# A planner learns what tile shapes cost: charges on TensorE, a 1e-9 moved to ScalarE, a new order

## The chip, the cores and the metric

The kernel runs on one core of one Trainium2 chip. The metric is the device time of one execution in microseconds. Five engines work side by side, each through its own queue in order: TensorE (PE; PEld is its weight load), VectorE (DVE), ScalarE (ACT), GpSimd (POOL) and SyncE (SP, which issues most DMAs). They wait for one another through semaphores only.

## The reference, cut to what matters

```python
# 1. attention: 4 batches, 8 heads, 576 rows, head size 64, rotary embedding on q and k
scores = scale * np.matmul(q_rot, k_rot.transpose(0, 1, 3, 2))
attn = np.exp(scores - np.max(scores, axis=-1, keepdims=True))
attn = attn / (np.sum(attn, axis=-1, keepdims=True) + 1e-09)
x = (attn @ v)                              # laid out as 2304 tokens x 512
# 2. a layer with SoLU and layer norm, 512 -> 1024 -> 512
h = x @ w_in
e = np.exp(h - h_max)
solu = h * (e / (np.sum(e, axis=-1, keepdims=True) + 1e-09))
x = ((solu - mu) / np.sqrt(var + 1e-06) * g_ln) @ w_out
# 3. experts: tokens with x @ w_skip > 0 go to the expert of their largest logit
out = x + gate * (np.maximum(x @ w1[e], 0.0) @ w2[e])
```

## The kernel before, in words

Every float32 product is made from two halves: a rounded high part and the rest, so one product is three matmuls (high x high, high x low, low x high). ScalarE makes the high part, VectorE the low one.

Attention goes over 16 pairs of heads (4 batches x 4). A pair loads q, k and v, applies the rotary embedding on GpSimd or VectorE (L475 to L487), transposes the result on TensorE (L503, L506), splits it (L532, L535) and has a DMA swap the halves of q (L560). Then it goes through 5 chunks of query rows (`chunk`). Chunks 0 to 3 hold 128 rows of both heads, chunk 4 the last 64 rows of each. For each head of a chunk: the scores (`score`, L595, 64-row tiles of TensorE, into one of two PSUM buffers S), their negated maximum (L598, VectorE), the exp with its sum (L601, ScalarE). Then, once for the chunk, VectorE adds 1e-9 to the sums (L610) and takes the reciprocal (L611), and each head's row block is scaled by it on ScalarE (L619), VectorE (L621) or GpSimd (L623). TensorE transposes the blocks (L661; for chunk 4 in 64-row tiles, L638), ScalarE or VectorE evict them (L668, L670), and TensorE multiplies by v (L700, 128 x 64 tiles, "pv").

The second layer goes over 18 tiles of 128 tokens (`solu`): w_in matmuls (L748), maximum, exp, product, statistics, a power on GpSimd (L777), the layer norm's scaling (L782, then L788 on ScalarE or L790 on VectorE or GpSimd), transposes (L802) and splits, w_out matmuls (L823), the output rows, and the routing of the tile's tokens, which ends in a scatter of rows by GpSimd (L899). The weights are turned into high and low parts on the way. When the last tile is routed, tables are made and a loop over expert tiles follows (L1053 to L1080), whose code is written by hand, outside the plan; two expert tiles of the fullest early expert are planned as filler for the end.

What sets the order: every step up to there is registered by `op(engine, kind, function, reads, writes, priority)` with a class `Plan`. `Plan.run` plays the steps on five engines: a step's duration comes from `COST`, the delay between engines from `LAT`, the buffers from `CAPS`; an engine that is free takes the ready step of lowest priority number whose buffers are free. The order in which it takes them is the program: `emit` writes it out, engine by engine. `TUNE` holds the priorities' offsets (`lead`, `sb`, `so`, `lt` and others) and lists that choose an engine for a step: `rp` (rotary embedding), `nr` (scaling: 0 GpSimd, 1 ScalarE, 2 VectorE), `ev` (eviction: 0 VectorE, 1 ScalarE), `ln` (layer norm: 0 GpSimd, 1 ScalarE, 2 VectorE), `xg`, `xs`, `le`, `wh`, `wl` (smaller copies). `BETWEEN` names the VectorE kinds that the plan lets start only when GpSimd isn't holding the data port they share, and `HOLDS` the GpSimd kinds that hold it. On the chip nothing of the plan is left but the order in each queue.

Of the kernel before, what the change touches and what calls it, by code (L numbers as in the profile page):

```python
# [9 lines left out]
F32 = mybir.dt.float32  # L10
# [4 lines left out]
AF = mybir.ActivationFunctionType  # L15
ALU = mybir.AluOpType
# [5 lines left out]
    "w_ld": (450, 1456), "c_ld": (2250, 1200), "w_1": 335, "w_2": 602, "w_r": 520, "w_add": 1250, "w_log": 663, "rope3": 1560, "ropev3": 790, "w_hi": 613, "w_lo": 663, "w_loP": 1225, "w_hiv": 400,  # L22
    "qk_ld": (450, 819), "v_ld": (2400, 910), "ropev": 680, "rope": 1393, "prep4": 430, "prep1": 107,
    "st_hi": 605, "st_lo": 700, "st_hi1": 160, "st_lo1": 230, "st_hi2": 278, "st_lo2": 447, "q2_ld": (1250, 1638),
    "score": 480, "score2": 960, "max": 665, "exp": 717, "rec": 278, "norm": 724, "normA": 667, "normv": 429, "h_lnA": 1130, "h_lnv": 723,
    "T10": 650, "DVE_ev5": 480, "ACT_ev5": 430, "T4": 436, "T1": 107, "ACT_ev4": 478, "DVE_ev4": 602, "DVE_ev1": 198, "ACT_ev1": 160, "pv": 2320, "x_hi2": 265, "x_lo2": 335, "pvs": 870,
    "DVE_ev1": 198, "x_hi": 160, "x_lo": 202, "mm3": 696, "mm1": 235, "h_max": 1140, "h_exp": 1120, "h_u": 1140, "h_bn": 600,
    "h_st": 805, "h_pow": 700, "h_mu": 70, "h_ln": 1190, "c_hi": 478, "c_lo": 602, "xs_ev": 478, "x_st": (1250, 730),
    "lg": 356, "g_sum": 120, "g_max": 80, "g_exp": 250, "g_hot": 927, "g_gate": 340, "rank": 140, "g_acc": 70, "g_ix": 477,
# [9 lines left out]
    'ld': 106.36,  # L39
    'ldv': 102.14,  # L40
    'rope': -9.86,
    'qk': 1.92,
    'sl': 0.88,
    'pvl': 6.39,
    'sper': 11.03,
    'hq': 31.3,
    'lt': -81.75,
    'rt': 5.62,
    'ew': 191.41,
    'olag': 1,  # L50
    'direct': 1,
    'c': -67.39,
    'lead': [136.53, 2.97, 6.06, 5, 9.68, -2.38, 8.75, 5.34, -1.45, -2.08, 8.42, 4.99, 0.81, 14.63, 7.23,
# [32 lines left out]
BETWEEN = {"w_1", "w_2", "w_hiv", "w_log", "normv", "h_lnv", "h_st", "h_mu", "g_hot", "g_ix"}  # L86
HOLDS = {"rope", "rope3", "norm", "w_add", "w_loP", "h_ln", "r_xP", "xf_loP"}
# [14 lines left out]
class Plan:  # L102
# [38 lines left out]

    def run(self):
        ops, lat = self.ops, self.lat
# [6 lines left out]
        room = {t: [(0, x) for x in range(n)] for t, n in self.caps.items()}  # L150
# [4 lines left out]
        rt = [0] * len(ops)  # L155
        ev = [(0, o.i) for o in ops if not o.nd]
        ev += [(t, -1) for t in busy.values()]
        heapq.heapify(ev)
        now, hw, dm = 0, 0, self.start.get("DMA", 0)
        held = free = 0  # L160
        seq = []
        while len(seq) < len(ops):
# [5 lines left out]
            for e, h in ready.items():  # L168
# [3 lines left out]
                while h:  # L172
                    x = heapq.heappop(h)
                    need = {}
                    for f in ops[x[1]].alloc:
                        need[f.tag] = need.get(f.tag, 0) + 1
                    if all(sum(y[0] <= now for y in room[t]) >= n for t, n in need.items()):
                        got = ops[x[1]]
                        break
                    skip.append(x)  # L180
# [12 lines left out]
                if not isinstance(c, tuple):  # L193
                    s0 = now
                    if o.kind in BETWEEN:
                        s0 = max(now, held)
                    elif o.kind in HOLDS:
                        s0 = max(now, free)
                    o.t1 = busy[e] = s0 + c * (2 if e == "PE" and now < self.warm else 1)
                    if o.kind in BETWEEN:  # L200
                        free = o.t1
                    elif o.kind in HOLDS:
                        held = o.t1
                elif e == "SP":
                    busy[e] = hw = max(hw, now) + c[0]
                    o.t1 = dm = max(dm, hw + 650) + c[1]
                    out = self.dma
                else:
                    busy[e] = now + c[0]
                    o.t1 = busy[e] + c[1]  # L210
# [31 lines left out]
def kern(ctx, tc, q, k, v, w_in, w_out, g_ln, w_skip, w_gate, w1, w2, cs, ids, out):  # L242
    nc = tc.nc
    P = 128
# [18 lines left out]
    eps = cst.tile([P, 4], F32, name="eps")  # L263
# [172 lines left out]
    def pair(n):  # L436
# [145 lines left out]
        def chunk(c):  # L582
# [26 lines left out]
            def rec(nx=nx):  # L609
                nc.vector.tensor_tensor(sr[:, 0:nx], sr[:, 0:nx], eps[:, 0:nx], op=ALU.add)  # L610
                nc.vector.reciprocal(sr[:, 0:nx], sr[:, 0:nx])  # L611

            op("DVE", "rec", rec, r=[(sr, x) for x in range(nx)], w=[(sr, "r")], pri=ps_)
# [705 lines left out]
```

## Time and profile before

| | us |
|---|---|
| three runs | 710.41, 710.58, 705.21 (median 710.41) |
| the profiled execution's own time | 709.91 |
| its span, first to last instruction | 708.0 |
| TensorE busy | 648.4 (92%) |
| VectorE busy | 512.4 (72%) |
| ScalarE busy | 369.9 (52%) |
| GpSimd busy | 251.6 (36%) |

The busy shares are means over stages that differ: attention alone at first, attention with the second layer in the middle, experts at the end. A matmul's end is modelled, so TensorE's pace is read from the starts of its instructions. The granted clock says how much of TensorE's full speed the chip allowed in a stretch; 0.5 is the lower level.

### The profile page before, as it was taken

The numbers are of one execution on the slowest core, as the hardware profiler recorded it, in microseconds if no ns is written. First come the engines' busy times: TensorE is split into PE (matmuls) and PEld (weight loads), VectorE is DVE, ScalarE is ACT, GpSimd is POOL, SyncE is SP. The second block draws the span as 40 slices with busy tenths as digits, with TensorE's granted clock in tenths as the row PEclk, the third lists the DMA queues.
The fourth block names the chain that finished last, engine by engine and source line by source line (L and its number), as shares of the span: only waits on it lengthen the run. The fifth ranks groups of instructions, "written<-read, shape, count | busy, mean of one in ns | idle before, by whom it ended". The sixth has DMA issues, their size and how long they took to land. (4 is left out here: it accounts for less than half of the span.)

```text
span 708.0 us, 12918 instructions
## 1 busy us (share of the span) xinstructions
PE 648.4 (92%) x4588; PEld 487.6 (69%) x4588; DVE 512.4 (72%) x1265; ACT 369.9 (52%) x845; POOL 251.6 (36%) x266
## 2 busy tenths in 40 slices
PE   2888978979999999999999999999999969898994
PEld 1655656757777777777776777777777757677773
DVE  5899889999888778888788779768677845224411
ACT  2777767678535556655475475855345421123311
POOL 5985735463214816205013403213112231421230
PEclk9998889999999999999999999999999989999998
DMA  4624334442212322111221201200136110440000
GB/s 136 171 79 140 87 96 117 124 112 80 62 33 54 88 50 62 36 49 37 53 73 31 67 1 45 64 19 1 23 74 175 45 45 16 160 178 31 18 32 11
DMA packets 42188, 49.10 MB, mean 69 GB/s; under 512 B 27508, under 2 KB 27636, under 8 KB 42112
## 3 DMA queue, kind: packets, MB, share of 16 engines
q1 hardware_dynamic: 39744, 44.43, 23.5%
q0 software_dynamic: 2368, 3.74, 1.7%
q8 instruction: 38, 0.62, 0.4%
q14 instruction: 38, 0.31, 0.2%
HBM read 38.50 MB, written 6.99 MB: 64 GB/s over the span
## 5 line engine op out<-in xcount | busy, mean ns | idle before, releaser
L601 ACT ACTIVATE P<-S,nm 128x576 f32<-128x576 f32 x144 | 106.5, 741 | 39.3 <-DVE nm L598 31.2
L598 DVE TENSOR_REDUCE nm<-S 128x1 f32<-128x576 f32 x144 | 106.4, 748 | 11.9 <-PE S L595 9.5
L823 PE MATMUL A<-woh,lh 128*128 128x512 f32 x288 | 110.6, 421 | 0.0
L595 PE MATMUL S<-k,qa 64*128 64x288 f32 x576 | 100.2, 324 | 4.0 <-ACT P L601 1.9
L661 PE MATMUL T<-ident,P 128*128 128x128 f32 x576 | 88.8, 287 | 11.3 <-ACT ptall L668 4.4
L700 PE MATMUL T<-ptall,vt 128*64 128x256 f32 (+2 forms) x960 | 95.5, 344 | 2.6 <-DVE qa L535 1.3
L661 PEld LDWEIGHTS T<-ident,P 128*128 128x128 f32 x576 | 67.1, 144 | 33.5 <-ACT ptall L668 7.2
L595 PE MATMUL S<-k,qb 64*128 64x288 f32 x384 | 83.5, 333 | 1.9 <-ACT P L601 1.7
L595 PEld LDWEIGHTS S<-k,qa 64*128 64x128 f32 x576 | 70.2, 191 | 18.6 <-issue 9.2
L700 PEld LDWEIGHTS T<-ptall,vt 128*64 128x64 f32 (+1 forms) x960 | 56.8, 140 | 33.5 <-issue 8.3
L668 ACT ACTIVATE ptall<-T 128x512 f32<-128x512 f32 (+1 forms) x117 | 57.2, 507 | 37.0 <-PE T L661 33.9
L623 POOL TENSOR_SCALAR P<-P,sr 128x576 f32<-128x576 f32 x43 | 36.3, 846 | 102.6 <-DVE sr L611 61.7
L595 PEld LDWEIGHTS S<-k,qb 64*128 64x128 f32 x384 | 57.0, 194 | 14.1 <-issue 5.9
L823 PEld LDWEIGHTS A<-woh,lh 128*128 128x128 f32 x288 | 54.7, 190 | 15.6 <-issue 4.6
L748 PE MATMUL S<-wih,xth 128*128 128x512 f32 x144 | 60.3, 419 | 0.0
L823 PE MATMUL A<-wol,lh 128*128 128x512 f32 x144 | 56.7, 394 | 0.0
L748 PE MATMUL S<-wih,xtl 128*128 128x512 f32 x144 | 56.4, 392 | 0.0
L748 PE MATMUL S<-wil,xth 128*128 128x512 f32 x144 | 56.3, 391 | 0.0
L475 POOL TENSOR_TENSOR rt<-raw,csq 128x576 f32<-128x576 f32 x23 | 33.6, 1462 | 62.0 <-PE T L506 40.2
L619 ACT ACTIVATE P<-P,sr 128x576 f32<-128x576 f32 x60 | 45.5, 775 | 14.3 <-DVE sr L611 12.1
L670 DVE COPY ptall<-T 128x512 f32<-128x512 f32 (+1 forms) x75 | 37.7, 518 | 10.2 <-PE T L661 8.8
L899 POOL DMA_INDIRECT srt<-gi,ix x18 | 19.6, 1091 | 70.7 <-DVE ix L896 38.5
(228 smaller groups left out, 1288.0 us busy)
## 6 DMA issues: line engine op xcount, KB each, us to landing
qb<-qa SPq DMA_DIRECT2D x30, 256.0 KB, 3.7
raw<-in_q SPq DMA_DIRECT2D x16, 288.0 KB, 2.9
raw<-in_k SPq DMA_DIRECT2D x16, 288.0 KB, 3.9
out<-xs SPq DMA_DIRECT2D x36, 128.0 KB, 2.4
s<-in_moe_w_in SPq DMA_DIRECT2D x8, 512.0 KB, 5.1
s<-in_moe_w_out SPq DMA_DIRECT2D x8, 512.0 KB, 3.7
st<-in_moe_w SPq DMA_DIRECT2D x8, 512.0 KB, 4.6
w1r<-in_moe_w SPq DMA_DIRECT2D x4, 1024.0 KB, 8.2
```

The lines of the kernel that those rows point to most:

```text
L475: e.tensor_tensor(t1[:, 0:NJ].rearrange("p j (e i) -> p j e i", e=2), raw.t.rearrange("p j (e i) -> p j e i", e=2), c, op=ALU.mult)
L595: nc.tensor.matmul(sp[:, bank, 0:288], lhsT=l, rhs=r_, start=first, stop=fin)
L598: nc.vector.tensor_reduce(nm[:, x:x + 1], sp.t[:, :, 0:288], AX.XY, ALU.max, negate=True)
L601: nc.scalar.activation(pt[:, x * S:(x + 1) * S].rearrange("p (a b) -> p a b", a=2), sp.t[:, :, 0:288], AF.Exp, bias=nm[:, x:x + 1], accum_ ...
L619: nc.scalar.activation(y, y, AF.Copy, scale=sr[:, x:x + 1])
L623: nc.gpsimd.tensor_scalar(y, y, sr[:, x:x + 1], 1.0, op0=ALU.mult, op1=ALU.mult)
L661: nc.tensor.transpose(tp.t[:w_, (y - g0) * P:(y - g0) * P + P], pt[:, y * P:y * P + w_], ident)
L668: nc.scalar.activation(ov, iv, AF.Copy)
L670: nc.vector.tensor_copy(ov, iv)
L700: nc.tensor.matmul(xp.t[64 * h:64 * h + 64, 0:M], lhsT=l, rhs=r_, start=(i == 0), stop=(i == 4))
L748: nc.tensor.matmul(hp[:, hf], lhsT=a, rhs=bb, start=(kc == 0 and y == 0), stop=(kc == KC - 1 and y == 2))
L823: nc.tensor.matmul(ob.t, lhsT=lh[:, a, kc], rhs=bb[:, kc], start=(kc == 0 and y == 0), stop=(kc == FC - 1 and y == 2))
```

## The change

Three things. The plan charges TensorE for a change of tile shape: `SHAPE` gives the kinds their shape (r: 64-row tiles, c: column tiles, m: full matmuls of the split weights, f: all others, the transposes), `CHANGE` the nanoseconds for going from one to the other, and where the tuned number `stick` is not 0, TensorE takes a ready step whose shape costs nothing ahead of the first ready one, if its priority number is at most `stick` higher. `BETWEEN` gains three kinds, `HOLDS` loses two that no step uses. The addition of 1e-9 to the softmax sums is an Identity activation with a bias operand on ScalarE. The costs and all of `TUNE` are drawn anew, and with them the order of the whole plan.

```diff
...
+    'stick': 0.5,
...
-    'ln': [1, 2, 0, 0, 2, 0, 0, 0, 2, 2, 2, 0, 0, 2, 1, 1, 1, 0],
+    'ln': [1, 0, 1, 2, 2, 1, 0, 2, 1, 2, 1, 1, 1, 1, 2, 1, 2, 1],
...
-BETWEEN = {"w_1", "w_2", "w_hiv", "w_log", "normv", "h_lnv", "h_st", "h_mu", "g_hot", "g_ix"}
-HOLDS = {"rope", "rope3", "norm", "w_add", "w_loP", "h_ln", "r_xP", "xf_loP"}
+BETWEEN = {"w_1", "w_2", "w_hiv", "w_lo", "w_log", "ropev", "ropev3", "normv", "h_lnv", "h_st", "h_mu", "g_hot", "g_ix"}
+HOLDS = {"rope", "rope3", "norm", "w_add", "w_loP", "h_ln"}
+
+SHAPE = {"score": "r", "score2": "r", "T10": "r", "pv": "c", "pvs": "c", "lg": "c", "mm3": "m", "mm1": "m", "rank": "m", "tab2": "m"}
+CHANGE = {"fm": -80, "fr": 94, "fc": 94, "mr": 178, "mc": 178, "rf": 92, "rm": 92, "rc": 92}
...
+                if e == "PE" and stick:
+
+                    rest = sorted(h)
+                    fit = [x for x in rest if self.fits(ops[x[1]], room, now)]
+                    same = [x for x in fit if CHANGE.get(last + SHAPE.get(ops[x[1]].kind, "f"), 0) <= 0]
+                    if fit:
+                        x = same[0] if same and same[0][0] <= fit[0][0] + stick else fit[0]
...
+                    if e == "PE":
+                        y = SHAPE.get(o.kind, "f")
+                        s0 += CHANGE.get(last + y, 0)
+                        last = y
...
             def rec(nx=nx):
-                nc.vector.tensor_tensor(sr[:, 0:nx], sr[:, 0:nx], eps[:, 0:nx], op=ALU.add)
                 nc.vector.reciprocal(sr[:, 0:nx], sr[:, 0:nx])
 
-            op("DVE", "rec", rec, r=[(sr, x) for x in range(nx)], w=[(sr, "r")], pri=ps_)
+            op("ACT", "s_eps", lambda nx=nx: nc.scalar.activation(sr[:, 0:nx], sr[:, 0:nx], AF.Identity, bias=eps[:, 0:1]),
+               r=[(sr, x) for x in range(nx)], w=[(sr, "e")], pri=ps_)
+            op("DVE", "rec", rec, r=[(sr, "e")], w=[(sr, "r")], pri=ps_)
```

Of the 144 entries of `nr` that are used, GpSimd has 43 before and 57 after, ScalarE 60 and 45, VectorE 41 and 42. Of the 128 evictions of four blocks ScalarE has 84 before and 73 after, VectorE 44 and 55. Of the 18 layer norms GpSimd has 8 before and 2 after, ScalarE 4 and 10, VectorE 6 and 6.

## Rows read from the trace of the kernel before

**Rows 1.** The page, part 1: busy us (share of the span) and instructions.
```profile
PE 648.4 (92%) x4588; PEld 487.6 (69%) x4588; DVE 512.4 (72%) x1265; ACT 369.9 (52%) x845; POOL 251.6 (36%) x266
```
**Rows 2.** Busy time by stretch: length, busy us by engine (instructions), granted clock, DMA share, GB/s.
```profile
40.00:80.00 40.00, 33.69 (x286) 23.41 (x284) 36.23 (x68) 29.49 (x72) 27.29 (x22) 0.87 0.36 110
80.00:120.00 40.00, 34.15 (x306) 23.52 (x306) 36.45 (x69) 30.66 (x78) 20.99 (x19) 0.91 0.40 104
280.00:360.00 80.00, 80.00 (x637) 59.91 (x636) 66.54 (x162) 44.20 (x107) 19.02 (x22) 1.00 0.21 52
560.00:580.00 20.00, 13.29 (x78) 10.15 (x77) 11.16 (x42) 6.25 (x13) 10.57 (x13) 0.92 0.16 40
```
**Rows 3.** TensorE's waits from 20 to 120 us: total us, times, longest.
```profile
PE T L661 <- ACT ptall L668: 3.7, 5, 1.1
```
**Rows 4.** TensorE's timeline: start us, us, what (first and last 64-row visit too).
```profile
14.57 0.60 PE L595 MATMUL S<-k,qa 64*128 64x288 f32 x1 [1.34 <-ACT k L532]
...
304.24 1.09 PE L661 MATMUL T<-ident,P 128*128 128x128 f32 x8
305.26 1.06 PE L595 MATMUL S<-k,qa 64*128 64x288 f32 x12
306.25 1.20 PE L661 MATMUL T<-ident,P 128*128 128x128 f32 x9
...
322.87 0.66 PE L661 MATMUL T<-ident,P 128*128 128x128 f32 x4
323.46 0.40 PE L595 MATMUL S<-k,qa 64*128 64x288 f32 x1
...
324.05 0.50 PE L823 MATMUL A<-woh,lh 128*128 128x512 f32 x1
...
508.77 0.52 PE L638 MATMUL T<-ident,P 64*128 64x64 f32 x10
```
**Rows 5.** Lines L610, L611: min/median/max ns; then L610's busy time by stretch.
```profile
L610 DVE TENSOR_TENSOR sr<-sr,eps x80: 139/154/1399, 20.0 to 496.7; 128x2 f32<-128x2 f32 x64, 128x1 f32<-128x1 f32 x16
...
L611 DVE RECIPROCAL sr<-sr x80: 163/166/167, 21.4 to 496.9; 128x2 f32<-128x2 f32 x64, 128x1 f32<-128x1 f32 x16
...
0.00:708.00 708.00, 28.20 (x80) 0.97 0.26 69
40.00:160.00 120.00, 11.86 (x24) 0.93 0.38 106
```
**Rows 6.** Timeline of all engines from 65.5 to 76 us.
```profile
67.30 1.31 DVE L610 TENSOR_TENSOR sr<-sr,eps 128x2 f32<-128x2 f32 x1
...
69.05 4.53 PE L700 MATMUL T<-ptall,vt 128*64 128x256 f32 x20 [1.27 <-DVE qa L535]
```
**Rows 7.** Groups of instructions by shape: busy us, mean ns | idle before.
```profile
L619 ACT ACTIVATE P<-P,sr 128x576 f32<-128x576 f32 x60 | 45.5, 775 | 14.3 <-DVE sr L611 12.1 <-DVE sr L610 2.0
L623 POOL TENSOR_SCALAR P<-P,sr 128x576 f32<-128x576 f32 x43 | 36.3, 846 | 102.6 <-DVE sr L611 61.7 <-ACT qa L532 7.9 <-DVE rt L866 7.1
L790 POOL TENSOR_SCALAR s<-s,st 128x1024 f32<-128x1024 f32 x8 | 9.6, 1203 | 2.2 <-DVE st L782 2.1
L871 ACT ACTIVATE rt<-rt,sc 128x8 f32<-128x8 f32 x18 | 5.3, 294 | 14.2 <-DVE sc L869 14.1
L788 ACT ACTIVATE s<-s,st 128x1024 f32<-128x1024 f32 x4 | 5.0, 1242 | 6.4 <-DVE st L782 6.4
L716 ACT ACTIVATE xth<-T 128x64 fp32r<-128x64 f32 x16 | 3.6, 223 | 1.8 <-PE T L700 1.6
```
**Rows 8.** Timeline from 569.5 to 583 us, TensorE and the others, at the plan's end.
```profile
569.59 0.16 DVE L782 SCALAR_TENSOR_TENSOR st<-st 128x1 f32<-128x1 f32 x1 [0.21 <-POOL st L778]
...
576.80 0.98 POOL L899 DMA_INDIRECT srt<-gi,ix  x1 [1.89 <-DMA srt<-gi,ix]
577.82 1.20 POOL L790 TENSOR_SCALAR s<-s,st 128x1024 f32<-128x1024 f32 x1
...
579.07 1.97 PE L802 MATMUL T<-ident,s 128*128 128x128 f32 x8 [4.35 <-POOL s L790]
```

More of the change, by code (lines that the diff above doesn't have):

```diff
@@ L21 @@
 COST = {
-    "w_ld": (450, 1456), "c_ld": (2250, 1200), "w_1": 335, "w_2": 602, "w_r": 520, "w_add": 1250, "w_log": 663, "rope3": 1560, "ropev3": 790, "w_hi": 613, "w_lo": 663, "w_loP": 1225, "w_hiv": 400,
+    "w_ld": (450, 1456), "c_ld": (2250, 1200), "w_1": 336, "w_2": 602, "w_r": 520, "w_add": 1240, "w_log": 663, "rope3": 1780, "ropev3": 860, "w_hi": 613, "w_lo": 590, "w_loP": 1225, "w_hiv": 400,
     "qk_ld": (450, 819), "v_ld": (2400, 910), "ropev": 680, "rope": 1393, "prep4": 430, "prep1": 107,
[L24 to L27, printed above, removed]
+    "st_hi": 494, "st_lo": 600, "st_hi1": 160, "st_lo1": 198, "st_hi2": 278, "st_lo2": 447, "q2_ld": (1250, 1638),
+    "score": 502, "score2": 900, "max": 665, "exp": 717, "rec": 166, "norm": 724, "normA": 667, "normv": 429, "h_lnA": 1130, "h_lnv": 723,
+    "s_eps": 170, "T10": 327, "DVE_ev5": 465, "ACT_ev5": 385, "T4": 436, "T1": 107, "ACT_ev4": 478, "DVE_ev4": 602, "DVE_ev1": 198, "ACT_ev1": 160, "pv": 2310, "x_hi2": 265, "x_lo2": 335, "pvs": 877,
+    "DVE_ev1": 198, "x_hi": 160, "x_lo": 202, "mm3": 692, "mm1": 232, "h_max": 1140, "h_exp": 1120, "h_u": 1140, "h_bn": 600,
     "h_st": 805, "h_pow": 700, "h_mu": 70, "h_ln": 1190, "c_hi": 478, "c_lo": 602, "xs_ev": 478, "x_st": (1250, 730),
-    "lg": 356, "g_sum": 120, "g_max": 80, "g_exp": 250, "g_hot": 927, "g_gate": 340, "rank": 140, "g_acc": 70, "g_ix": 477,
+    "lg": 356, "g_sum": 120, "g_max": 80, "g_exp": 250, "g_hot": 927, "g_gate": 340, "rank": 64, "g_acc": 70, "g_ix": 477,
     "i_sc": (1145, 2000), "early": 2220, "s_hi": 947, "s_lo": 1130, "reg": 100, "i_gm": (1330, 2000), "tiny": 70,
@@ L38 @@
 TUNE = {
[L39 to L49, printed above, removed]
+    'ld': 223.09,
+    'ldv': 109.51,
+    'rope': -4.23,
+    'qk': 1.85,
+    'sl': 0.97,
+    'pvl': 6.24,
+    'sper': 9.82,
+    'hq': 39.91,
+    'lt': -204.54,
+    'rt': 6.21,
+    'ew': 159.86,
+    'stick': 0.5,
     'olag': 1,
     'direct': 1,
-    'c': -67.39,
-    'lead': [136.53, 2.97, 6.06, 5, 9.68, -2.38, 8.75, 5.34, -1.45, -2.08, 8.42, 4.99, 0.81, 14.63, 7.23,
[26 rows of a table removed]
+    'c': -67.43,
+    'lead': [141.78, 1.69, 6.41, 5.16, 9.38, -2.25, 16.91, 3.12, -1.34, 2.06, 8.53, -2.72, -2.24, 11.44, 1.42,
[26 rows of a table added]
 }
@@ L140, in op, with fits @@
         return o
+    @staticmethod
+    def fits(o, room, now):
+        need = {}
+        for f in o.alloc:
+            need[f.tag] = need.get(f.tag, 0) + 1
+        return all(sum(y[0] <= now for y in room[t]) >= n for t, n in need.items())
     def run(self):
@@ L160, in run @@
         held = free = 0
+        last, stick = "f", self.tune.get("stick", 0)
         seq = []
@@ L171, in run @@
                 skip, got = [], None
-                while h:
+                if e == "PE" and stick:
[4 more added lines that the diff above has]
+                        x = same[0] if same and same[0][0] <= fit[0][0] + stick else fit[0]
+                        rest.remove(x)
+                        got = ops[x[1]]
+                        h[:] = rest
+                while h and got is None and not (e == "PE" and stick):
                     x = heapq.heappop(h)
[L174 to L177, printed above, removed]
+                    if self.fits(ops[x[1]], room, now):
                         got = ops[x[1]]
@@ L262, in kern @@
     g_sb = cst.tile([P, FC], F32, name="g_sb")
-    eps = cst.tile([P, 4], F32, name="eps")
+    eps = cst.tile([P, 1], F32, name="eps")
     nc.vector.memset(eps, 1e-9)
```

50 rows, old and new, of the table TUNE are left out of this document.

## The prediction

> **What bounds the kernel now.** The first view to read is the page's share of busy time: TensorE 92%, VectorE 72%, ScalarE 52% [rows 1]. That is an average over stages with different limits, so the second view is the table of busy time by stretch [rows 2]. It shows three regimes. From 280 to 360 us TensorE is busy for all 80.00 us at full granted clock and VectorE for 83%: there only less work on TensorE shortens anything. From 40 to 120 us TensorE is busy for 33.69 and 34.15 of 40 us, VectorE for 36.23 and 36.45, and the granted clock is 0.87 and 0.91 on average, that is, partly at the lower of the two levels (1.2 against 2.4 GHz). There TensorE waits for the softmax chain and then also runs slowly. From 560 to 580 us, where the second layer's last tile ends, TensorE is busy for 13.29 of 20 us at 0.92. Behind it comes the loop over experts, which the diff doesn't touch. So the change can win in three ways: fewer or cheaper shape changes in the full stretch, a shorter chain in the front, a better end of the plan. The third view, the list of waits in the front, says who ended TensorE's idle time from 20 to 120 us: the longest entry is an eviction on ScalarE, 3.7 us in 5 waits [rows 3].
>
> **Shape changes on TensorE (term A).** The plan now charges 92 to 178 ns for going into or out of the 64-row shape (scores) and 94 to 178 ns for going into the 64-column shape. Does the chip charge that? Two rows of the PE timeline answer: a visit with two scores (12 matmuls) takes 0.99 us to the start of the next shape, a visit with one (6 matmuls) takes 0.59 [rows 4]. So six matmuls cost 0.40 and leaving costs 0.19. Entering costs too: eight transposes followed by a score take 1.02 us from start to start, four take 0.59, so four more cost 0.43 and entering 0.16 [rows 4]. A visit avoided is worth about 0.35 us. On the timeline I count 122 visits to the 64-row shape, from the first score at 14.57 to the last ten 64-row transposes at 508.77 [rows 4]; 77 of them hold one operation. The charge alone changes nothing on the chip; it works through the new rule `stick`, which lets TensorE take a ready operation of a free shape ahead of one that is up to 0.5 more urgent. It can only join scores that are ready together, and a score is ready only when one of two S buffers is free, so most of the 77 will stay. I take 12 visits fewer: 12 x 0.35 = 4.2, **-4 us**. Bounds: 0 (none joined) and -15 (122 down to 80, two to a visit, 42 x 0.35).
>
> The Trainium skill, TensorEngine Tiling (Array Packing), section Key Properties, says that changing the tiling mode drains TensorE. The 0.19 us on leaving a score visit agrees with that; the page has no price.
>
> **The 1e-9 moves from VectorE to ScalarE (term B).** Removed: 80 additions on VectorE, 28.2 us in all, a mean of 0.35 us [rows 5]. The spread says what they are: 139 ns at least, 154 in the middle, 1399 at most, while the reciprocal right behind takes 163 to 167 every time [rows 5]. Without the long ones they would cost 80 x 0.154 = 12.3, so 15.9 us is time held up by GpSimd. The timeline shows one in place: the addition that begins at 67.30 lasts 1.31 us; behind it in VectorE's queue stands the last split of q, and TensorE's pv group waits 1.27 us for that split [rows 6]. That group then takes 4.53 us at the lower clock level, which follows the idle time. What that level costs is seen from eight transposes, 1.09 us at 304.24 and 1.97 at 579.07 [rows 4, 8]: nearly half of the 4.53 is lost, and as much of the transposes behind it. So this one held addition cost 1.27 plus some 3, together about 4.5.
>
> Added: 80 Identity calls on ScalarE, in its queue behind the exp of the same chunk, with all the queued evictions and exps behind them; TensorE waits for those. No row shows this call. The nearest: an eviction of 64 columns takes 223 ns, an exp of 8 columns with a bias operand 294 [rows 7]. The s_eps call has two columns and a bias operand, so the two are its bounds, and I take the lower, since the call is the smallest of the three. ScalarE gains 80 x 0.22 = 17.6 us (to 23.5). By the lists in the diff it also loses 15 scalings (0.775 each) and gains 6 layer norms (1.242 each), -11.6 + 7.5 [rows 7], and loses 11 four-block evictions. Its sum rises by some 10 us over the span, which it has to spare from 280 us on (44 of 80 us busy [rows 2]). In the front, 24 of the calls lie between 40 and 160 us, where the additions cost VectorE 11.86 us [rows 5]; 24 x 0.22 = 5.3 goes onto ScalarE. VectorE's wait for ScalarE stays, at the reciprocal in place of the addition and one call later; behind it in VectorE's queue stand maxima, evictions and splits, as before. The latency of one chain (exp, addition, reciprocal, scaling) stays about what it was without a hold, and the hold is gone. Of the front I count one place like that at 67 us as won: **-5 us**. Bounds: 0, and -20 (11.86 us of VectorE's time all on the path, with the clock lost over 40 to 120 us, 0.13 x 40 + 0.09 x 40 = 8.8).
>
> The Trainium skill, SBUF — State Buffer, section Who interferes with whom, says that a VectorE instruction with two SBUF inputs contends with a GpSimd instruction that reads SBUF, and one with a single SBUF input outside the two-port modes does not. The trace agrees: 139 to 1399 ns for the addition, 163 to 167 for the reciprocal. Against the change stands the Trainium skill, ScalarE: Activation LUTs, section Rules for kernel authors, which puts additions on VectorE rather than ScalarE; the section What ACT_TABLE_LOAD costs gives about 280 ns for a call with a pointer bias, which by an estimate from that page makes 80 x 0.28 = 22.4 us of ScalarE's time. That alone would leave the sum as it is.
>
> **The new order: the end of the plan (term D).** The last tile's layer norm had its inputs at 569.59 + 0.16 us, but it runs on GpSimd at 577.82, since GpSimd's queue first issues the row scatters of earlier tiles, the last of them after 1.89 us of waiting for the one before [rows 8]. TensorE's transposes start at 579.07 after 4.35 us idle, and eight of them take 1.97 us [rows 8]. If the lower level lasts about as long as the idle time did, 4.3 us at little over half pace, 2.1 us more are lost: 4.35 + 2.1 = 6.5 us. In the diff the last entry of `ln` goes from 0 (GpSimd) to 1 (ScalarE), where a layer norm takes 1.242 us: it would end at about 571.0, while TensorE still has other work until 579.07 - 4.35 = 574.7. What is late next is the tile's w_out group and its routing, which follow as before. **-6 us**, bounds 0 (another wait takes its place) and -6.5.
>
> **The rest of the new order.** 14 more scalings go to GpSimd (0.846 each [rows 7]), 11.8 us more that can hold VectorE, less six layer norms (1.203 each) that leave it. BETWEEN now knows three more VectorE operations that wait on GpSimd; this costs nothing at run time and makes the order truer. HOLDS loses two names that no operation bears. But every list was drawn again, and a new order has new stalls that the old one doesn't have. I price them with the place at 67 us, 4.5: **+5 us**, bounds 0 and +12 (three such places, less the one counted as won).
>
> **Sum.** Against the profiled execution's own time of 709.91 us (span 708.0 and 1.9 around it, 0.5 under the median of 710.41): 709.9 - 4 - 5 - 6 + 5 = **700 us**.
>
> **Rivals.**
> - *Given back.* The new order's stalls eat terms A and B; only the end of the plan is won, 709.9 - 6 + 3 = 707 us. For it: nothing ties the new lists to the chip's waits, and the front has held additions in only a few places. Against it: VectorE loses 28 us of work in any order.
> - *The rule joins nothing.* Scores become ready one at a time, so visits stay near 122 and term A is nil: 704 us. For it: two S buffers, 77 single visits. Against it: scores of one chunk have the same priority.
> - *ScalarE becomes the bound of the front (slower).* The 24 calls between 40 and 160 us [rows 5] stand in order before evictions and exps that TensorE waits for already [rows 3]. If each holds the queue 0.29 us, and waits for exp's sum as long again, that is 24 x 0.58 = 14 us on the path, with two half-clock places at some 3 more each; with A and D as above 709.9 + 14 + 6 - 10 = 720, and half of it on the path gives 710. It decides from the point where a call costs ScalarE more than the 0.35 us (28.2 / 80) that it saves VectorE. Against it: ScalarE is busy for 74 and 77% there [rows 2], and loses scalings and evictions.
>
> **How the numbers follow.** Two runs of this kernel can't be told apart within 1%. Forecast 0.53 (692 to 704, at 700); given back 0.27 (703 to 713); rule joins nothing, the rest as forecast, 0.08 (702 to 707); ScalarE bound 0.12 (710 to 722). Faster by over 1%, below 703.3: 0.49 of the first, 0.02 of the second, 0.03 of the third, 0.54. Slower, above 717.5: 0.07 of the last and 0.04 of the second, should it miss its 713, 0.11. Within 1%: 0.35. The range leaves out the ScalarE case beyond 714 and, below, terms A and B at more than twice their size: 688 to 714.
>
> **What would show it.** A: the count of score visits falls from 122 to about 110, and TensorE's busy time by some 4 us. B: VectorE's busy time falls by over 20 us; the new ScalarE rows have a mean of 170 to 295 ns; the granted clock of 40 to 120 us rises above 0.9. D: no idle of over 2 us on TensorE between 560 and 585 us. If the score visits stay and VectorE's relief shows without TensorE's busy share in the front rising, the forecast is wrong by terms A and B; if ScalarE's share of 40 to 120 us rises above 85%, the last rival holds.

## The result: 690.3 us, the profile after, and where the time went

The changed kernel takes 690.27 us (median of four runs, 688.96 to 692.64) against 709.9 before (four runs, 705.21 to 710.58): a ratio of 0.974, 95% interval 0.969 to 0.979. The profiled execution took 688.96, its span is 687.2. The forecast was 700, the range 688 to 714. In the jobs of the experiments below the kernel before ran 65 times more, 702.53 to 712.68, median 707.4; so its four runs here lie on the high side, and some 2 or 3 of the 20 us may be no gain.

The lines of the code moved: L595 is now L618 (scores), L601 L624 (exp), L611 L633 (reciprocal), L661 L685, L700 L724, L802 L826, L899 L923, L1041 L1065, L1156 L1180, and L635 is the new call, s_eps.

The page after, part 1, as [rows 1]:

```profile
PE 634.6 (92%) x4588; PEld 483.6 (70%) x4588; DVE 483.7 (70%) x1199; ACT 372.7 (54%) x899; POOL 259.6 (38%) x278
```

TensorE has the same 4588 matmuls and 13.8 us less busy time, VectorE 28.7 us less. ScalarE rises by only 2.8: its 80 new calls are nearly paid for by scalings and evictions that left it. Busy time by stretch after, as [rows 2] (the fourth stretch is longer than there and ends where the expert tables begin):

```profile
40.00:80.00 40.00, 35.12 (x320) 25.24 (x319) 33.16 (x69) 30.72 (x82) 23.73 (x20) 0.91 0.39 113
80.00:120.00 40.00, 36.48 (x358) 26.03 (x354) 36.29 (x72) 36.75 (x100) 30.37 (x27) 1.00 0.46 129
280.00:360.00 80.00, 79.91 (x630) 61.68 (x626) 64.76 (x162) 46.96 (x122) 28.84 (x32) 1.00 0.26 56
540.00:582.00 42.00, 39.14 (x227) 30.27 (x225) 29.14 (x132) 11.70 (x28) 13.03 (x17) 1.00 0.13 33
```

From 40 to 120 us TensorE is busy for 71.6 us of 80 (67.8 before), at 0.91 and 1.00 of full clock (0.87 and 0.91 before). The middle is as full as it was. The end of the plan now runs at full clock.

Where did 20 us go? The first matmul of the tables (out T, in ident and tv) marks the end of the plan. TensorE's timeline, before and then after:

```profile
601.59 0.97 PE L1156 MATMUL T<-ident,tv 128*128 128x28 f32 x8
```

```profile
581.67 0.97 PE L1180 MATMUL T<-ident,tv 128*128 128x28 f32 x8
```

It comes 19.9 us earlier; what follows takes 106.4 us before and 105.5 after. Up to that point, busy time by stretch, before and after:

```profile
0.00:200.00 200.00, 166.22 (x1358) 118.88 (x1359) 176.58 (x357) 135.08 (x321) 109.74 (x110) 0.96 0.39 108
200.00:540.00 340.00, 336.97 (x2524) 255.55 (x2523) 267.61 (x708) 188.72 (x444) 97.49 (x110) 0.99 0.20 49
540.00:601.59 61.59, 54.66 (x294) 41.67 (x293) 39.22 (x157) 19.57 (x37) 17.15 (x21) 0.94 0.23 52
```

```profile
0.00:200.00 200.00, 168.18 (x1326) 123.89 (x1327) 159.05 (x332) 137.57 (x344) 120.33 (x121) 0.97 0.39 108
200.00:540.00 340.00, 337.83 (x2629) 258.85 (x2628) 266.42 (x690) 197.40 (x485) 99.09 (x115) 1.00 0.23 55
540.00:581.67 41.67, 38.81 (x223) 29.94 (x222) 28.89 (x132) 11.70 (x28) 13.03 (x17) 1.00 0.13 33
```

A stretch's length less TensorE's busy time is its idle time. The clock's part is worked out from the same view cut into pieces of 2 us: TensorE's busy time in a piece times what the granted clock lacks to 1, summed. What is left is TensorE's own time, its work at full clock. For four kernels that the text comes back to (idle + clock, us):

| up to the tables | before | after | after, addition back on VectorE | before, last layer norm on ScalarE |
|---|---|---|---|---|
| front, 0 to 200 | 33.8 + 7.1 | 31.8 + 6.5 | 38.4 + 5.9 | 34.7 + 5.0 |
| middle, 200 to 540 | 3.0 + 1.6 | 2.2 + 0.0 | 3.9 + 0.0 | 2.7 + 1.6 |
| end, 540 to the tables | 6.9 + 2.2 | 2.9 + 0.0 | 3.0 + 3.1 | 2.7 + 0.0 |
| TensorE's own time | 546.9 | 538.3 | 539.9 | 546.1 |
| tables begin at | 601.59 | 581.67 | 594.15 | 592.70 |

From before to after, idle time and clock give 2.6 us in the front, 2.4 in the middle, 6.3 at the end, and TensorE's own time 8.6.

Own time: TensorE's timeline after holds 105 visits to the 64-row shape, 17 fewer than before. In units of one score (six matmuls) or ten 64-row transposes, singles fell from 77 to 49, doubles went from 37 to 41, visits of three from 7 to 15 (before, one more holds four). Chunk 4's score is one planned step of twelve matmuls and counts as two here; in planned steps, visits of one fell from 92 to 58. Going into the column shapes (pv and the router's logits) hardly changed: 61 times before, 59 after, up to the tables. All changes between 64-row, column and full shape together fell from 320 to 276. A visit of three, and what follows it:

```profile
305.65 0.40 PE L618 MATMUL S<-k,qb 64*128 64x288 f32 x1
...
307.04 0.95 PE L724 MATMUL T<-ptall,vt 128*64 128x64 f32 x20
```

Start to start it is 1.39 us, 0.40 more than the visit of two in [rows 4], which was 0.40 more than a visit of one.

The 1e-9. The new call, the reciprocal behind it, and VectorE's wait between them (min/median/max ns; then us in total, times, longest):

```profile
L635 ACT ACTIVATE sr<-sr,eps x80: 281/295/385, 26.1 to 477.5; 128x2 f32<-128x2 f32 x64, 128x1 f32<-128x1 f32 x16
```

```profile
L633 DVE RECIPROCAL sr<-sr x80: 143/156/168, 26.4 to 478.3; 128x2 f32<-128x2 f32 x64, 128x1 f32<-128x1 f32 x16
```

```profile
DVE sr L633 <- ACT sr L635: 12.4, 14, 3.7
```

The call costs 23.40 us in all, 293 ns each, with little spread; the addition it replaces had taken up to 1399 [rows 5]. VectorE waits for it 14 times in 80, 12.4 us in all. TensorE's largest wait from 20 to 120 us is now for an exp, 5.6 us in 5 waits, where [rows 3] had an eviction:

```profile
PE S L618 <- ACT P L624: 5.6, 5, 2.9
```

The last layer norm. The timeline of all engines, as [rows 8]:

```profile
556.78 0.15 DVE L806 SCALAR_TENSOR_TENSOR st<-st 128x1 f32<-128x1 f32 x1
...
558.16 1.23 ACT L812 ACTIVATE s<-s,st 128x1024 f32<-128x1024 f32 x1
...
559.46 0.99 POOL L923 DMA_INDIRECT srt<-gi,ix  x1 [2.45 <-DVE gi L910]
...
559.98 1.04 PE L826 MATMUL T<-ident,s 128*128 128x128 f32 x8
```

It runs 1.2 us after its inputs (8.1 before), while GpSimd still issues scatters behind it, and the eight transposes follow without idle time, at full clock.

### The profile page after: what moved, and what is told of

Its sections match the earlier page's. It is cut to its first block, busy times and chain, and to the rows that moved or that the text cites. A ratio compares the mean times of both kernels' runs of the same rounds, so it can differ in the third digit from the quotient of the medians.

```text
span 687.2 us, 12857 instructions
## 1 busy us (share of the span) xinstructions
PE 634.6 (92%) x4588; PEld 483.6 (70%) x4588; DVE 483.7 (70%) x1199; ACT 372.7 (54%) x899; POOL 259.6 (38%) x278
## 5 line engine op out<-in xcount | busy, mean ns | idle before, releaser
L624 ACT ACTIVATE P<-S,nm 128x576 f32<-128x576 f32 x144 | 106.7, 742 | 45.5 <-DVE nm L621 44.2
L847 PE MATMUL A<-woh,lh 128*128 128x512 f32 x288 | 108.0, 416 | 0.0
L618 PE MATMUL S<-k,qa 64*128 64x288 f32 x576 | 96.5, 322 | 5.3 <-ACT P L624 3.2
L724 PE MATMUL T<-ptall,vt 128*64 128x256 f32 (+2 forms) x960 | 92.9, 337 | 0.8 <-DVE qa L558 0.8
L685 PE MATMUL T<-ident,P 128*128 128x128 f32 x576 | 87.9, 285 | 5.9 <-ACT ptall L692 2.0
L647 POOL TENSOR_SCALAR P<-P,sr 128x576 f32<-128x576 f32 x57 | 45.8, 809 | 111.2 <-DVE sr L633 94.7
L618 PE MATMUL S<-k,qb 64*128 64x288 f32 x384 | 81.4, 333 | 5.1 <-ACT P L624 5.1
L685 PEld LDWEIGHTS T<-ident,P 128*128 128x128 f32 x576 | 67.6, 145 | 24.2 <-issue 6.9
L618 PEld LDWEIGHTS S<-k,qa 64*128 64x128 f32 x576 | 70.4, 192 | 17.7 <-ACT P L624 6.5
L724 PEld LDWEIGHTS T<-ptall,vt 128*64 128x64 f32 (+1 forms) x960 | 55.7, 138 | 30.9 <-issue 6.5
L692 ACT ACTIVATE ptall<-T 128x512 f32<-128x512 f32 (+1 forms) x110 | 51.2, 491 | 37.2 <-PE T L685 36.8
L618 PEld LDWEIGHTS S<-k,qb 64*128 64x128 f32 x384 | 57.3, 196 | 16.6 <-ACT P L624 7.6
L694 DVE COPY ptall<-T 128x512 f32<-128x512 f32 (+1 forms) x82 | 44.2, 552 | 11.8 <-PE T L685 11.3
L801 POOL TENSOR_TENSOR st<-st,half 128x1 f32<-128x1 f32 x18 | 10.7, 595 | 79.6 <-DVE st L798 47.0
L923 POOL DMA_INDIRECT srt<-gi,ix x18 | 19.5, 1085 | 55.1 <-DVE sc L893 13.7
```

Of the source, the lines that this page charges most:

```text
L618: nc.tensor.matmul(sp[:, bank, 0:288], lhsT=l, rhs=r_, start=first, stop=fin)
L624: nc.scalar.activation(pt[:, x * S:(x + 1) * S].rearrange("p (a b) -> p a b", a=2), sp.t[:, :, 0:288], AF.Exp, bias=nm[:, x:x + 1], accum_ ...
L647: nc.gpsimd.tensor_scalar(y, y, sr[:, x:x + 1], 1.0, op0=ALU.mult, op1=ALU.mult)
L685: nc.tensor.transpose(tp.t[:w_, (y - g0) * P:(y - g0) * P + P], pt[:, y * P:y * P + w_], ident)
L692: nc.scalar.activation(ov, iv, AF.Copy)
L694: nc.vector.tensor_copy(ov, iv)
```

## Experiments

"Ratio" is to the kernel before, run on the same chip in the same job, with the 95% interval. The changed kernel was not run again in these jobs; its ratio is 0.974 (0.969 to 0.979).

| kernel | us | ratio |
|---|---|---|
| after, addition back on VectorE | 701.5 | 0.993 (0.990 to 0.996) |
| before, addition on ScalarE | 705.2 | 0.997 (0.9949 to 0.9996) |
| before, last layer norm on ScalarE | 701.9 | 0.993 (0.990 to 0.995) |
| before, both edits | 698.5 | 0.988 (0.986 to 0.991) |
| after, no addition at all | 690.8 | 0.977 (0.975 to 0.980) |
| after, addition as an immediate | 692.2 | 0.978 (0.974 to 0.981) |
| after, `stick` 0 | 728.2 | 1.031 (1.027 to 1.035) |
| after, with the lists of before | 724.0 | 1.024 (1.021 to 1.027) |
| after, visits split (bf16 operands) | 696.5 | 0.983 (0.979 to 0.987) |
| its control | 694.7 | 0.982 (0.978 to 0.986) |
| after, visits split (the scores' operands) | 701.5 | 0.993 (0.989 to 0.996) |
| its control | 698.3 | 0.986 (0.982 to 0.990) |

The theory: three gains that add up (fewer visits, no held addition, the last layer norm off GpSimd). The rival: the new order as such is better, and the named parts are beside the point.

**1. The addition back on VectorE, in the new order.** The planner still places s_eps on ScalarE, so the order of everything else stays, but the step emits nothing.

```diff
-    eps = cst.tile([P, 1], F32, name="eps")
+    eps = cst.tile([P, 4], F32, name="eps")
...
             def rec(nx=nx):
-                nc.vector.reciprocal(sr[:, 0:nx], sr[:, 0:nx])
-
-            op("ACT", "s_eps", lambda nx=nx: nc.scalar.activation(sr[:, 0:nx], sr[:, 0:nx], AF.Identity, bias=eps[:, 0:1]),
+                nc.vector.tensor_tensor(sr[:, 0:nx], sr[:, 0:nx], eps[:, 0:nx], op=ALU.add); nc.vector.reciprocal(sr[:, 0:nx], sr[:, 0:nx])
+
+            op("ACT", "s_eps", lambda: None,
```

> The changed kernel's order on every engine, but VectorE adds the 1e-9 right before the reciprocal, and ScalarE's 80 calls are gone. Theory (the place of the addition counts: it is held up by GpSimd on VectorE): VectorE's busy time rises by 20 to 28 us, some additions take over 1 us again, and the time is 694 to 700 us. Rival (all of the gain is the new order, the place of the addition is worth nothing): 688 to 692 us.

701.5 us, a little over the 694 to 700 of the theory: 11 of the 20 us are gone. The additions are held again, by line (min/median/max ns):

```profile
L633 DVE TENSOR_TENSOR sr<-sr,eps x80: 138/151/1373, 25.4 to 488.1; 128x2 f32<-128x2 f32 x64, 128x1 f32<-128x1 f32 x16
```

That GpSimd holds them can be read from the timeline. One of them, with the GpSimd instruction beside it:

```profile
114.51 1.41 POOL L498 TENSOR_TENSOR rt<-raw,csq 128x576 f32<-128x576 f32 x1
114.61 1.33 DVE L633 TENSOR_TENSOR sr<-sr,eps 128x2 f32<-128x2 f32 x1
```

The addition begins 0.10 us after the GpSimd instruction and ends 0.02 us behind it. All the long ones look like this: 20 of the 80 take over 250 ns here and 19 of 80 in the kernel before, and each of them ends 4 to 23 ns after the GpSimd instruction that was running when it began. Not every addition beside a GpSimd instruction is held: a few of 140 to 179 ns have one running all along.

The third column of the table of stages above says where it is lost: 6.6 us more idle time in the front, 1.7 in the middle. The clock's 3.1 at the end is a drop that other profiles of this order show too, at half that size (1.4 to 1.7), so it isn't put down to the addition.

**2. The addition on ScalarE, in the old order.**

```diff
             def rec(nx=nx):
-                nc.vector.tensor_tensor(sr[:, 0:nx], sr[:, 0:nx], eps[:, 0:nx], op=ALU.add)
+                nc.scalar.activation(sr[:, 0:nx], sr[:, 0:nx], AF.Identity, bias=eps[:, 0:1])
                 nc.vector.reciprocal(sr[:, 0:nx], sr[:, 0:nx])
```

> The order of the kernel before on every engine, but ScalarE adds the 1e-9 in place of VectorE. Theory: the hold at 67 us and the half-clock stretch behind it go, 703 to 707 us. Rival 1 (worth nothing without a new order): 709 to 711. Rival 2 (ScalarE's queue becomes the bound of the front, since a call takes 0.3 us there): 712 or more, and ScalarE's share of 40 to 120 us above 85%.

705.2 us, 2 less than before; the interval of the ratio just leaves out 1. The call costs ScalarE the same (276 to 355 ns) and VectorE's busy time falls to 485.2 us as it does after. But VectorE now waits. Its waits in this kernel:

```profile
DVE sr L611 <- ACT sr L610: 39.2, 55, 2.2
```

39.2 us in 55 waits, against 12.4 in 14 in the changed kernel. In the old order the reciprocal stands in VectorE's queue where the addition stood, right behind the exp, and the call has to fit between: the time that VectorE no longer works, 27 us, it now waits. So the same edit is worth 2 us in one order and 11 in the other.

It is tempting to put the difference down to these waits, but TensorE doesn't show them. In the front and middle its idle time and clock come to 40.9 us in this kernel (40.6 in experiment 4, which has the same call), as little as in the changed kernel (40.5). What differs is the kernel that the edit starts from: with the addition on VectorE they are 45.5 us in the old order (43.9 in experiment 3) and 48.2 in the new one. That speaks for held additions having cost TensorE less in the old order, rather than for VectorE's new waits costing more; but single profiles scatter by several us in these stretches (experiment 6's has 47.0), so the cause of the difference between 2 and 11 isn't shown.

**3. The last layer norm on ScalarE, in the old order.**

```diff
-            z = PR["ln"][i]
+            z = 1 if i == NTILE - 1 else PR["ln"][i]
```

> The order of the kernel before, but the last tile's layer norm runs on ScalarE in place of GpSimd, nothing else. Theory (it stood behind GpSimd's row scatters): the 4.35 us of idle time on TensorE and the half-clock stretch behind it go, 702 to 705 us. Rival (the tile's routing or another wait is as late): 708 to 711 us.

701.9 us, 5.4 less than before, at the edge of the 702 to 705 of the theory. ScalarE's and TensorE's timeline there:

```profile
569.68 1.23 ACT L788 ACTIVATE s<-s,st 128x1024 f32<-128x1024 f32 x1
...
572.22 1.03 PE L802 MATMUL T<-ident,s 128*128 128x128 f32 x8
```

The transposes begin at 572.22 instead of 579.07, without idle time, and take 1.03 us instead of 1.97 [rows 8]. In the table of stages the end falls from 6.9 + 2.2 to 2.7 + 0.0, that is, by 6.5 before rounding.

**4. Both edits, in the old order.** Experiments 2 and 3 together.

> The order of the kernel before with both single edits: ScalarE adds the 1e-9, and ScalarE has the last tile's layer norm. Theory (they act in different stages and add up): 0.9973 x 0.9925 = 0.990 of the kernel before, 699 to 702 us. Rival (what the front wins is lost again in the full stretch): 0.9925, 702 to 704 us.

698.5 us; the ratio of 0.988 is that of the two alone, multiplied (0.997 x 0.993 = 0.990), within the interval. Against experiment 3 (0.993) the addition is worth 3 us here. So the two named edits are worth 9 us without a new order; the rest, 10 by the ratio of 0.974 and 8 by that of experiment 5 below (0.977), came only with it.

**5. No addition at all, in the new order.** This kernel leaves out the 1e-9; s_eps emits nothing and the reciprocal reads the sums as they are.

```diff
-            op("ACT", "s_eps", lambda nx=nx: nc.scalar.activation(sr[:, 0:nx], sr[:, 0:nx], AF.Identity, bias=eps[:, 0:1]),
+            op("ACT", "s_eps", lambda: None,
```

> The changed kernel's order, with the 1e-9 left out: the reciprocal reads exp's sum. (Each sum holds exp(0) = 1, so that 1e-9 is below its last digit.) ScalarE loses 23.4 us of calls, of which 8.2 between 40 and 160 us, and VectorE's reciprocals wait for exp alone. Theory (ScalarE's calls lie mostly beside other work, since TensorE is full from 160 us on): 685 to 690 us. Rival (they stand on the path of the front, as the 12.4 us of waits of the reciprocal on them suggest): 678 to 684 us.

690.8 us, the same as the changed kernel, and just over the 685 to 690 of the theory. The page says that the calls are gone, 80 instructions and 13.9 us of ScalarE's busy time fewer than after:

```profile
PE 636.3 (92%) x4588; PEld 484.7 (70%) x4588; DVE 483.2 (70%) x1199; ACT 358.8 (52%) x819; POOL 260.7 (38%) x278
```

In this order the 80 calls lie beside other work and cost nothing, and what the addition on VectorE cost in experiment 1 is won back by moving it. 13.9 / 80 is 0.17 us each, less than the 0.29 of a call's record. ScalarE's timeline of the changed kernel shows why:

```profile
104.38 0.31 ACT L635 ACTIVATE sr<-sr,eps 128x2 f32<-128x2 f32 x1
104.56 0.76 ACT L624 ACTIVATE P<-S,nm 128x576 f32<-128x576 f32 x1
```

The next exp starts 0.18 us after the call, before the call has ended.

**6. The addition as an immediate, in the new order.**

```diff
-            op("ACT", "s_eps", lambda nx=nx: nc.scalar.activation(sr[:, 0:nx], sr[:, 0:nx], AF.Identity, bias=eps[:, 0:1]),
+            op("ACT", "s_eps", lambda nx=nx: nc.scalar.activation(sr[:, 0:nx], sr[:, 0:nx], AF.Copy, bias=1e-9),
```

> The changed kernel's order, with ScalarE's call as a Copy with an immediate bias in place of an Identity with a bias operand. Theory: the call shortens from 295 to about 200 ns, 80 x 0.095 = 7.6 us less on ScalarE, 2 of them in the front: 687 to 690.5 us, not to be told from the changed kernel. Rival (calls on the path of the front): 684 to 687 us.

The call is 92 ns shorter (line, min/median/max ns):

```profile
L635 ACT ACTIVATE sr<-sr x80: 188/203/234, 25.9 to 482.8; 128x2 f32<-128x2 f32 x64, 128x1 f32<-128x1 f32 x16
```

The time, 692.2 us (686.1 to 695.6; 687 to 690.5 had been expected), can't be told from that of the changed kernel. That agrees with experiment 5: a call that costs nothing can't be made cheaper.

**7. The rule off.** The plan is made anew from the new lists and charges, without the rule.

```diff
-    'stick': 0.5,
+    'stick': 0,
```

> The changed kernel with stick at 0: TensorE takes the first ready step again, whatever its shape; the charges and all lists stay, so the order is planned anew from the same lists. Theory (the rule joins scores): 64-row visits rise from 105 to about 120, and the time to 695 to 700 us. Rival (the lists are fitted to one order and any disturbance costs, or the visits don't matter): visits and time don't go together, say 105 to 110 visits and over 700 us, or 120 visits and 688 to 692 us.

728.2 us, slower than before the change and than either expectation. Visits are back at 122 (76 single, 38 double, 8 triple). But visits are not what makes the 38 us above the changed kernel. The tables begin at 622.41; against the changed kernel TensorE is idle for 25.0 us more (6.8 in the front, 5.2 in the middle, 13.0 at the end) and loses 10.0 more to the clock; its own time is 5.8 higher. TensorE's longest waits from 540 us to the tables (us in total, times, longest):

```profile
PE T L1065 <- DMA xr<-out,mt: 8.3, 1, 8.3
PE T L913 <- DVE sc L908: 4.2, 1, 4.2
```

The filler at the end waits 8.3 us for its rows to be gathered. The lists were drawn together with the rule; without it they give another order.

**8. The old lists in the new planner.** All of `TUNE` as before, with `stick` 0.5, the new costs and charges, `BETWEEN` and s_eps.

```diff
     'stick': 0.5,
...
-    'ln': [1, 0, 1, 2, 2, 1, 0, 2, 1, 2, 1, 1, 1, 1, 2, 1, 2, 1],
+    'ln': [1, 2, 0, 0, 2, 0, 0, 0, 2, 2, 2, 0, 0, 2, 1, 1, 1, 0],
...
```

> The changed kernel's plan (charges, stick 0.5, ScalarE's add, new durations) with the lists and offsets of the kernel before. Theory (the rule by itself joins scores): about 105 to 110 64-row visits, and 6 to 7 us less of shape changes; with the end of the old lists (last layer norm on GpSimd) 697 to 706 us. Rival (an order that the lists weren't drawn for has new stalls, as without stick): visits fall, but idle time and lost clock on TensorE grow by over 10 us together, 710 to 735 us.

724.0 us, in the range of the rival, but with 122 visits (74 single, 42 double, 6 triple): over the old lists the count is that of the kernel before, so neither expectation had the visits right. The loss has the same look, TensorE's longest wait from 540 us on:

```profile
PE T L1065 <- DMA xr<-out,mt: 13.1, 1, 13.1
```

Of the orders that ran, only that of rule and lists together has 105 visits, and only it and the old order with the last layer norm on ScalarE (experiments 3 and 4) have a good end.

**9. Visits split on purpose.** In the new order an 8-column matmul of the full shape goes ahead of the second head's scores in each chunk. It writes into eight columns of the scores' buffer that nothing reads; 64 are added, and visits go from 105 to 130. The control has the same matmul in the 64-row shape, which splits nothing. First with bf16 operands:

```diff
-                def score(hh_=hh_, sp=sp):
+                def score(hh_=hh_, sp=sp, x=x):
+                    if x:
+                        nc.tensor.matmul(sp[:, 1, 504:512], lhsT=ones[0:P, :], rhs=ones[0:P, 0:8], start=True, stop=True)
```

> The changed kernel's order, with one tiny full-shape matmul (8 columns, into a part of the scores' buffer that nothing reads) ahead of the scores of each chunk's second head, 64 in all. Where the two heads' scores were joined in one visit to the 64-row shape, it splits the visit. Theory (a visit costs about 0.35 us of TensorE's time where TensorE is full): some 35 to 45 visits more than 105, and 10 to 17 us more than the changed kernel, 700 to 708 us. Rival (a visit's price is hidden or is that of the added matmuls alone, 64 x 0.02 = 1.3 us): 690 to 693 us, like the control.

In the control the operands are `ones[64:, :]` and `ones[64:, 0:8]`.

> The control: the same 64 tiny matmuls at the same places, but in the scores' own 64-row shape, so that no visit is split. Both theories: 689 to 693 us, and 105 visits as in the changed kernel.

696.5 and 694.7 us, where 700 to 708 and 689 to 693 had been expected: the added matmul splits 25 visits, not 35 to 45, and the control costs something. Both medians lie above the changed kernel's, but the intervals of the three ratios meet. Locally a split pair takes 1.30 us to the next shape and a joined pair with the control's matmul 1.11, against 0.99 without either. The control isn't free, and it changes the data type in the middle of a visit, so both were repeated on the scores' own operands.

```diff
+                        nc.tensor.matmul(sp[:, 1, 504:512], lhsT=qa[:, 0:P], rhs=kt[:, 0, 1, 32:40], start=True, stop=True)
```

> As e10, but the 64 tiny matmuls take the scores' own operands (all 128 rows of q and k, 8 columns), so that only the tile shape differs from the scores' and not the data type too. About 25 of them split a visit (130 visits in e10's trace). Theory (a visit costs 0.35 us of TensorE's time): a split pair of scores takes 1.3 us to the next shape where a joined one takes 0.99, and the time is 3 to 9 us above the control's. Rival (no price but the added matmuls'): the time is the control's within 1.5 us.

In the control they are `qa[64:, 0:P]` and `kt[64:, 0, 1, 32:40]`.

> The control of e12: the same 64 tiny matmuls on the scores' own operands in the scores' own shape (64 rows). Both theories: a joined pair of scores with the tiny matmul inside takes 1.00 to 1.05 us, and the time is 688 to 692 us, the changed kernel's.

701.5 and 698.3 us, 3.2 apart, with intervals that still overlap; 3 to 9 had been expected, and 688 to 692 for the control. A split pair on TensorE's timeline, with the transposes that follow it (L620 is the scores there, L617 the added matmul):

```profile
332.60 0.38 PE L620 MATMUL S<-k,qa 64*128 64x288 f32 x1
...
333.17 0.27 PE L617 MATMUL S<-k,qa 128*128 128x8 f32 x1
333.38 0.40 PE L620 MATMUL S<-k,qa 64*128 64x288 f32 x1
...
333.96 0.66 PE L875 MATMUL T<-ident,xs 128*128 128x128 f32 x4
```

And a pair of the control:

```profile
339.59 0.40 PE L620 MATMUL S<-k,qa 64*128 64x288 f32 x1
...
340.09 0.17 PE L617 MATMUL S<-k,qa 64*128 64x8 f32 x1
...
340.69 0.33 PE L891 MATMUL T<-ident,s 128*128 128x128 f32 x1
```

Split, the pair takes 1.36 us (median of 13: 1.38), joined 1.10. So a split costs 0.28 us locally, and the 8-column matmul 0.11 even in the scores' own shape and type. That is more than was expected of the control: 64 x 0.11 = 7 us, which is most of what it lies above the changed kernel. The 3.2 us between the two kernels aren't the price of the 25 splits alone: at the other 39 places the added matmul splits nothing, but has another shape than in the control.

## Why the prediction held, point by point

**What bounds the kernel.** The three stretches where the change could win, a full TensorE, the front and the end, all gave something. The sum was right in sign and within its range, but 10 us short: 690.3 lies below the 692 at which the forecast's own case ended, and 2 us above the end of the wider range, which allowed for terms A and B at more than twice their size.

**Term A, shape changes: -4 predicted, about twice that measured.** TensorE's own time fell by 8.6 us. What was mis-sized is the 12 visits: 17 were saved. "Most of the 77 will stay" held, 49 did (the 77 "hold one operation" only if chunk 4's score counts as two; in planned steps 92 did), and so did the reason given, two S buffers: of the 15 visits of three in the new order, seven hold a score and chunk 4's double score, seven hold two scores and ten transposes, and only one holds three scores. Visits with two scores that each take a buffer rose from 23 to 42.

At the predicted 0.35 a visit, 17 are 6.0 us. All ten profiles without the added matmuls bear out that the fall goes with the visits: with 122 (before, experiments 2, 3, 4, 7 and 8) the own time is 544.1 to 547.9 us, mean 546.3; with 105 (after, experiments 1, 5 and 6) it is 536.9 to 539.9, mean 538.4, whatever the addition or the end did. That is 7.9 us for 17 visits, 0.46 each. The four with 105 share one order, though, so something else of that order could be in it; against the two other orders of the new planner (544.1 and 545.1) it is 6.2, 0.36 each.

One such thing can be counted: there are 44 changes of shape fewer in all, 10 more than the 34 of 17 visits, since TensorE more often goes straight from the 64-row to a column shape (29 times, 23 before) and goes into the column shapes twice less. At the 0.16 to 0.19 us a change of [rows 4], 44 are 7.0 to 8.4 us, an estimate that would cover the fall. Experiment 9 says less: a split costs 0.28 locally, 0.20 in own time (549.5 against 544.5, 25 visits) and 0.13 in the time of the whole (3.2 us). So the price of a visit lies between 0.13 and 0.46, with the predicted 0.35 inside, and why an added visit cost less than a saved one is open. The rival that the rule joins nothing fell for this kernel, but with the lists of before the count stays at 122 (experiment 8), so the step "it works through the new rule" was only half of it.

**Term B, the addition: -5 predicted, -11 measured in the order it runs in.** That GpSimd held the addition is confirmed by the ends of the long additions in experiment 1, and that the hold costs time by its medians: 701.5 us against 690.3, and against 690.8 with no addition (by the ratios, 13 and 11). The term was sized by one place, and more places counted. In the old order it is 2 to 3 us (experiments 2 and 4). The profiles of after and experiment 1 give 7.7 us of idle time and clock in the front and middle (40.5 against 48.2), but single profiles are not that sharp there: the one of experiment 6, the slowest of its six runs, has 47.0. The call lasts 293 ns, not 220: the upper of the two bounds, and the reason given for the lower, that the call is the smallest of the three, was wrong. Without the bias operand it takes 203 in the middle (experiment 6, where the function differs too), so the operand counts for more than the columns. The queue is held for only 0.17 to 0.18 us of it (experiment 5). The Trainium skill, ScalarE: Activation LUTs, section What ACT_TABLE_LOAD costs, had it at about 280, and the trace agrees with 281 to 385. It doesn't matter to the time (experiment 5), and where that page's section Rules for kernel authors puts additions on VectorE, the measurement decides otherwise here: 11 us.

**Term D, the end of the plan: -6 predicted, -6.3 measured** in the changed kernel and -6.5 in experiment 3 (5.4 in its medians). Mechanism, place and size were right, the lower clock behind the idle time included.

**The rest of the new order: +5 predicted, nothing measured once the addition has moved.** This step failed. With the addition left on VectorE, the new order does cost more in the front and middle: 48.2 us of idle time and clock, against 45.5 and 43.9 (before, experiment 3). But with the call on ScalarE the new order has 40.5 and the old one 40.9 and 40.6 (experiments 2 and 4). As far as these profiles go, the stalls that the new order brought are gone with the held additions. So terms B and the rest, 0 together in the forecast, gave 45.5 - 40.5 = 5.0 us.

Together: -8.6 - 5.0 - 6.3 = -19.9, and 0.9 after the tables, against 687.2 - 708.0 = -20.8 of the spans. The forecast had -4, 0 and -6; the 10 us that it was short are 4.6 in A and 5.0 in the price of the new order. Each is from one profile per kernel, and one drop of the clock is worth 1.5, so terms under 2 us aren't told apart, in the front and middle not even larger ones (experiment 6). The profiled run of the kernel before lies 2.5 us above the median of its 65 later runs, so the gain is nearer 17 us than 20, and some 2.5 us of these terms belong to that one run.

**The rivals.** Given back: it named stalls that eat A and B and a time of 707; with the call on ScalarE the front and middle lost no more in the new order than in the old. ScalarE as the bound of the front: its share of 40 to 120 us rose to 84% (30.72 + 36.75 of 80), near the 85% that was named, but TensorE's share rose with it, and without the calls the time is the same (experiment 5).

What isn't settled: which of the lists makes scores ready together, since no run changed only some of them; and what the redrawn costs and the new entries of `BETWEEN` do by themselves.

## What to carry to other kernels

Price a moved operation in the order it will run in: the same move was worth 2 to 3 us in the old order and 11 in the new one. A wait of the engine that was relieved need not be a wait of the engine that bounds the kernel: VectorE waited 39.2 us for the new call in the old order, and TensorE lost no more in the front and middle than in the new one. Ahead of the last tile of a stage, look at what an in-order queue must issue first: one layer norm behind GpSimd's scatters cost 5 to 6 us, a third of the whole change, and one entry of a list mended it. A planner's rules and the lists drawn with them are one thing; either changed alone made this kernel 2 to 3% slower than before, in part through a transfer at the end for which TensorE waited 8 to 13 us.

## What the runs showed of the hardware that was not expected

A VectorE addition on two columns, held by GpSimd, ends 4 to 23 ns after GpSimd's instruction does, up to 1.4 us after it began ([rows 5], experiment 1). A ScalarE call on one or two columns takes 281 to 385 ns with its bias in a tile and 188 to 234 with an immediate, and the next call can start 0.18 us after it began (experiment 5). An 8-column matmul between scores delays what follows by 0.11 us, in the scores' shape and type as well as in bf16. It has a weight load of its own, 182 ns at least, about what a score's takes in the changed kernel (a mean of 192 with qa). By line in the last control (min/median/max ns):

```profile
L617 PEld LDWEIGHTS S<-k,qa x64: 182/183/331, 16.2 to 476.8; 64*128 64x128 f32 x64
L617 PE MATMUL S<-k,qa x64: 163/270/372, 16.4 to 476.8; 64*128 64x8 f32 x64
```
